# Split first products, three-part sums and a guarded softmax in a convolution and maxout kernel

## The chip, the cores and the metric

The kernel runs on one core of a Trainium2 chip. The metric is the device time of one execution in microseconds (us). TensorE (PE in the profile) multiplies matrices, with its weight loads (PEld) beside it; VectorE (DVE) does elementwise work and reductions, ScalarE (ACT) activations and copies out of PSUM; GpSimd (POOL) and SyncE (SP) mostly issue transfers.

## The reference, cut to what matters

There are 8 x 4160 tokens of 192 features, in 8 heads of 24. Each token has 7 taps of weights per head, and a mixture of the last 7 tokens is formed with the softmax of these weights. Then comes a maxout layer with 1024 hidden columns.

```python
w = exp(weight_gen - max(weight_gen)); w = w / (sum(w) + 1e-9)     # 7 taps
y[s, h] = sum over k of w[s, h, k] * x_padded[s + k, h]            # 6 rows of zeros ahead
out = maximum(y @ w1, y @ w2) @ w_out                              # 192 -> 1024 -> 192
```

## The kernel before

**Layout.** Each of the 128 partitions holds 260 consecutive tokens, called columns. They form 17 batches: sixteen of 16 columns and one of 4. A batch is cut into units: four units of 4 columns in batches 0 and 1 (units 0 to 7), two of 8 columns later (units 8 to 35; unit 36 has 4). A unit of n columns gives n tiles of hidden work for TensorE, 260 in all. Tiles are taken in groups of two up to tile 16 and of three after that.

**Softmax.** No maximum is subtracted. For each batch, `exp_sum` (ACT, L135) makes exponentials, `red` (DVE, L147) sums the 7 taps, `ln` (ACT, L151) takes the logarithm, `shift` (DVE, L156) subtracts it from the weights, and `weights` (ACT, L167) takes the exponentials of the result, as bf16.

**Mixture.** `mul` (DVE, L182) multiplies 7 shifted views of x by the weights of one piece (4 or 8 columns) into `m_t`. For units 0 to 7, `sum_transpose` (PE, L248) adds the taps and transposes them in one go, by matmuls with an identity matrix, and ACT copies the result out (L255). From unit 8 on, `adds` (DVE, L198, L204, L207) adds the taps, a DMA transpose on SP (L216) turns the unit around, and a one-column copy on POOL (L224, tile `gate`) waits for its landing, with the next loads of x and of weights queued behind it on POOL. Stores of results that were held back are issued on SP right behind a transpose.

**Maxout.** max(a, b) = a + relu(b - a), so the weights are prepared as `wd` = w2 - w1 (`w_diff`, L584 to L591) and `w10` = w1 @ w_out. `hid_tile` (PE, L299) makes the differences of a tile, `relu` (ACT, L309) takes them out of PSUM, `out_first` and `out_second` (PE, L351, L339) add both products, `evac` (ACT, L395) copies the results and SP stores them (L409, the last one at L386 on SP and ACT).

**Order.** The schedule is manual: each engine works through the instructions in the order in which the program writes them. In the long stretch, `extra` puts DVE's work beside tiles: `mul`, then `adds` with a `beside` step ahead of the additions. A unit at the start of a batch has the three parts of a `shift` there, the other has two parts of a `red`. ACT's softmax steps come when a tile is reached: the table `due` is filled from defaults and from the table `AT` (an entry `('l', 8, 0): 95` places `ln` of batch 8 at tile 95; `X` is `exp_sum`, `W` is `weights`). Long steps can be put off by one group unless the group is in `NOW`.

**Start.** SP loads batch 0's weights, the halo (the six columns ahead), columns 0 to 3 of x, the first halves of w1 and w2, columns 4 to 7, then the rest. `mul(0, 0)` waits for columns 0 to 3; PE meanwhile runs `keep_warm` (L615, matmuls whose result is not used). The loads of columns 8 to 15 on POOL wait for `mul(0, 0)`.

Of the kernel before, what the change touches and what calls it, by code (L numbers as in the profile page):

```python
# [9 lines left out]
FP32 = mybir.dt.float32  # L10
# [13 lines left out]
def kernel(  # L24
# [19 lines left out]
    CPP = B * S // P  # L44
    RPB = P // B
    G = D // H
    assert RPB * CPP == S
# [27 lines left out]
    consts = ctx.enter_context(tc.tile_pool(name="consts", bufs=1))  # L75
    pwg = ctx.enter_context(tc.tile_pool(name="pwg", bufs=4))
    pxb = ctx.enter_context(tc.tile_pool(name="pxb", bufs=2))
    pe_ = ctx.enter_context(tc.tile_pool(name="pe", bufs=2))
    psm = ctx.enter_context(tc.tile_pool(name="psm", bufs=3))
    pm = ctx.enter_context(tc.tile_pool(name="pm", bufs=1))  # L80
    pen = ctx.enter_context(tc.tile_pool(name="pen", bufs=2))
    py = ctx.enter_context(tc.tile_pool(name="py", bufs=2))
    pyt = ctx.enter_context(tc.tile_pool(name="pyt", bufs=6))
    prd = ctx.enter_context(tc.tile_pool(name="prd", bufs=7))
    first_ps = ctx.enter_context(ExitStack())
    ps = {k: first_ps.enter_context(tc.tile_pool(name="pps_" + k, bufs=2, space=bass.MemoryType.PSUM))
          for k in ("h", "o")}

    def later_ps():

        first_ps.close()
        for k in ("ab", "c", "r"):
            ps[k] = ctx.enter_context(tc.tile_pool(name="pps_" + k, bufs=1, space=bass.MemoryType.PSUM))

    wg_ts, xb_ts, e_ts, s_ts, en_ts, y_ts, yt_ts = {}, {}, {}, {}, {}, {}, {}

# [38 lines left out]
    def part(b, i, of):  # L137
# [3 lines left out]
        return slice(h0, h1), h0 * K, [[K, h1 - h0], [1, K]]  # L141

    def red(b, i=0, of=1):
        if i == 0:
            s_ts[b] = psm.tile([P, BATCHES[b][1] * H], FP32, name="sum_t", tag="sum")
        hs, at, ap = part(b, i, of)
        nc.vector.reduce_sum(out=s_ts[b][:, hs], in_=_sub(e_ts[b], at, ap), axis=AX.X)  # L147

    def ln(b, i=0, of=1):
        s_t = s_ts[b][:, part(b, i, of)[0]]  # L150
        nc.scalar.activation(out=s_t, in_=s_t, func=AF.Ln)  # L151

    def shift(b, i=0, of=1):
        hs, at, ap = part(b, i, of)
        w_t = _sub(wg_ts[b], at, ap)
        nc.vector.tensor_tensor(out=w_t, in0=w_t, in1=_sub(s_ts[b], hs.start, [[1, hs.stop - hs.start], [0, K]]),  # L156
                                op=ALU.subtract)

    def weights(b, o):

        w = dict(pieces(b))[o]
        if b not in en_ts:
            en_ts[b] = pen.tile([P, 16 * WGC * 2], BF16, name="en_t", tag="en")
        J = 2 if w == 4 and b < 2 else 1
        N = w * H // J
        for j in range(J):
            nc.scalar.activation(  # L167
                out=_sub(en_ts[b], (o * WGC + j * N * K) * 2, [[2 * N, K], [2, N], [1, 2]]),
                in_=_sub(wg_ts[b], (o * H + j * N) * K, [[1, K], [K, N], [0, 2]]), func=AF.Exp,
            )  # L170


    def mul(b, o):

        n = dict(pieces(b))[o]
        if n == 4 and b < 2:
            m_out = _sub(m_t, K * o * D, [[64, 2], [P, K * 6], [1, 64]])
            x_in = _sub(xb_ts[b], o * D, [[2 * D, 2], [D, K], [1, 2 * D]])
        else:
            m_out = m_t[:, K * o * D:K * (o + n) * D]  # L180
            x_in = _sub(xb_ts[b], o * D, [[D, K], [1, n * D]])
        return nc.vector.tensor_tensor(  # L182
            out=m_out, in0=x_in,
            in1=_sub(en_ts[b], o * WGC * 2, [[2, K * n * H], [0, G // 2], [1, 2]]),
            op=ALU.mult,
        )
# [51 lines left out]

    def sum_transpose(u, taps=range(K)):

        b, o, n = UNITS[u]
        assert n == 4
        yps = ps["r" if "r" in ps else "o"].tile([P, 1024], FP32, name="yps", tag="op")
        for k in range(6):
            for t in taps:
                for r in range(2):
                    at = (K * o + t * n) * D + k * P
                    nc.tensor.matmul(  # L248
                        yps[:, r * 512 + k * 64:r * 512 + (k + 1) * 64],
                        lhsT=m_t[half(r), at:at + P], rhs=ident[half(r), half(r)],  # L250
                        start=(k == 0 and t == taps[0]), stop=(t == taps[-1]),
                        skip_group_check=True,
                    )
        yt = pyt.tile([P, 8 // 2 * 3 * P], BF16, name="yt", tag="yt")
        yt_of[u] = nc.scalar.copy(out=_sub(yt, 0, [[64, 2], [P, 6], [1, 64]]),  # L255
                                  in_=_sub(yps, 0, [[512, 2], [64, 6], [1, 64]]))
        yt_ts[u] = yt
# [119 lines left out]
    def evac(p, n):  # L377
# [20 lines left out]
        for q in range(p, p + n):  # L398
            u, i, _ = column(2 * q)
            if NU - 7 <= u < NU - 1 and i % 2:  # L400
                stores.append((nc.sync, place(q)[0] - 1, [4 * D, 2], [1, 2 * D]))
            elif u < NU - 7 and i == UNITS[u][2] // 2 - 1:
                stores.append((nc.sync, place(q)[0] - i, [1, 2 * (i + 1) * D]))
            if u == NU - 1:
                stores.append((nc.sync, place(q)[0], [2 * D, 2], [1, D]))
# [104 lines left out]
    msk = consts.tile([P, 1], FP32, name="msk")  # L510
    gate = consts.tile([P, 1], FP32, name="gate")
    o_last = consts.tile([P, 2 * D], FP32, name="o_last")

    with tc.tile_pool(name="pstage", bufs=1) as pstage:
# [57 lines left out]
        for o in (0, 4, 8, 12):  # L572
            weights(0, o)
        nc.vector.tensor_copy(out=xb_ts[0][:, PAD * D:(PAD + 4) * D],
                              in_=xs[:, PAD * D:(PAD + 4) * D])
        first_mul = mul(0, 0)
        w1 = {kind: pstage.tile([P, w], BF16, name="w1" + kind)
              for kind, w in (("E", F), ("T", HF))}

        nc.scalar.copy(out=w1["E"][:, 0:HF], in_=ws["E", 0][:, 0:HF])  # L580
        def w_diff(h, copy):

            c0 = slice(h * HF, (h + 1) * HF)
            nc.vector.tensor_tensor(out=wd[:, c0], in0=ws["E", 1][:, c0], in1=ws["E", 0][:, c0],  # L584
                                    op=ALU.subtract)
            copy(out=wd_at(1, 2, h, 0, HF), in_=wd[0:64, c0])
            copy(out=wd_at(0, 1, h, 0, HF), in_=wd[64:P, c0])
            if h == 0:
                nc.vector.tensor_tensor(out=wd[:, 2 * HF:3 * HF], in0=ws["T", 1], in1=ws["T", 0],
                                        op=ALU.subtract)  # L590
            copy(out=wd_at(1 - h, 1 + h, h, 0, HF), in_=wd[half(h), 2 * HF:3 * HF])  # L591
# [19 lines left out]

        def keep_warm(times):

            for _ in range(times):
                nc.tensor.matmul(warm[:, 0:512], lhsT=ident, rhs=_sub(ident, 0, [[0, 4], [1, P]]),  # L615
                                 start=True, stop=True, skip_group_check=True)

        keep_warm(30)
        w_diff(0, nc.scalar.copy)
        nc.vector.tensor_copy(out=xb_ts[0][:, (PAD + 4) * D:(PAD + 8) * D], in_=xs[:, (PAD + 4) * D:])  # L620
        behind(first_mul, load_x(0, 8, 4))
        load_x(0, 12, 4)
# [4 lines left out]

        sum_transpose(0)
        keep_warm(8)
        mul(0, 4)  # L630


        nc.scalar.copy(out=w1["T"], in_=ws["T", 0])  # L633
# [7 lines left out]
        relu(rd, 1, 1)  # L641
        w_diff(1, nc.vector.tensor_copy)
        sum_transpose(1)
        red(1)
# [51 lines left out]

    pout = ctx.enter_context(tc.tile_pool(name="pout", bufs=1))
    o_t.append(pout.tile([P, 24 * D], FP32, name="o_t", tag="o"))
# [5 lines left out]
    def end_of_1():  # L704
# [15 lines left out]

    NOW = (22, 28, 40, 49, 106)
    AT = {
# [6 lines left out]
        ('W', 3, 0): 22,  # L729
        ('l', 8, 0): 95,  # L730
        ('l', 11, 0): 144,
        ('l', 12, 0): 162,
        ('l', 5, 0): 45,
    }
    due = {}
# [26 lines left out]
    def extra(t):  # L762
# [14 lines left out]
        if s == 8 + later and b + 2 < NB:  # L777
            adds(b + 1, 8, beside=lambda i, of: red(b + 3, i, 2) if b + 3 < NB and i < 2 else None)
        if k == n // 4 - 1 and 7 < u + 1 < NU:
            transpose(u + 1)  # L780

    def steps(g, tiles):
# [3 lines left out]
        for t in tiles:  # L786
            extra(t)

    out_room(OUTS[3])
    go = relay(out_first(OUTS[3]))  # L790
# [3 lines left out]
    for g in range(4, len(GROUPS)):  # L794
        if GROUPS[g][1] == 3 and "c" not in ps:
            later_ps()
        tiles = [t for t in range(GROUPS[g][0], sum(GROUPS[g])) if t >= 16]
        if g == 9:
            behind(relu_of[16], load_x(3, 0, 8))
# [4 lines left out]
        else:  # L804
            hidden(g, OUTS[g], beside=lambda: steps(g, tiles))
    rest_of_results(OUTS[-1])

# [28 lines left out]
```

## Time and profile before

| what | value |
|---|---|
| three timed runs | 409.34, 409.50, 410.65 us; median 409.5 us |
| the profiled execution's own time | 410.25 us |
| its span, first to last instruction | 408.4 us |
| granted TensorE clock | full (1.00) |
| PE busy | 398.9 us (98%) |
| DVE busy | 371.7 us (91%) |
| ACT busy | 357.1 us (87%) |
| POOL busy | 72.5 us (18%) |

The span covers the instructions, and 1.85 us of the profiled execution lie around it (410.25 - 408.4). Busy shares are averages over stages: the start (to about 50 us), the long stretch of equal groups, and the end after DVE's last addition at 378.5 us.

### The profile page before, as it was taken

What the parts mean: (1) busy time and instruction counts of PE and PEld (TensorE: products, weight loads), DVE (VectorE), ACT (ScalarE), POOL (GpSimd) and SP (SyncE); (2) the same over time, 40 slices, a digit from 0 to 9 for tenths busy, and PEclk for the clock granted to TensorE, in tenths of its full rate; (3) what the DMA queues carried; (4) which work ended last, traced back from release to release, by engine and by line L of the source; (5) the groups of instructions that cost most, each with busy time, mean ns of one, the idle gap of its engine ahead of it and who ended that gap; (6) DMA issues with size and microseconds to landing.
All of it is one profiled execution on the core that took longest, in us unless ns stands there. A gap on an engine that the chain in (4) does not pass through costs nothing.

```text
span 408.4 us, 16153 instructions
## 1 busy us (share of the span) xinstructions
PE 398.9 (98%) x7422; PEld 317.6 (78%) x7422; DVE 371.7 (91%) x216; ACT 357.1 (87%) x424; POOL 72.5 (18%) x101
## 2 busy tenths in 40 slices
PE   7899999999999999999999999999999999999996
PEld 2589989777777777777877777777778777777796
DVE  4999999999999999999999999999999999999000
ACT  6799899999899998898998999998999988988872
POOL 0311012212222112121211122220122220210000
PEclk9999999999999999999999999999999999999999
DMA  8958399767658674976786588478648647654514
GB/s 242 218 125 219 75 186 167 168 165 173 147 113 237 151 167 105 244 201 69 234 203 84 123 248 202 65 243 180 128 109 239 169 68 237 154 127 111 145 55 142
DMA packets 62785, 65.70 MB, mean 161 GB/s; under 512 B 47711, under 2 KB 51679, under 8 KB 62718
## 3 DMA queue, kind: packets, MB, share of 16 engines
q1 hardware_dynamic: 54334, 40.54, 36.7%
q0 software_dynamic: 8240, 24.04, 29.9%
q8 instruction: 58, 0.95, 1.0%
q10 hardware_dynamic: 144, 0.10, 0.1%
q14 instruction: 9, 0.07, 0.1%
HBM read 35.96 MB, written 25.56 MB: 151 GB/s over the span
## 4 chain that ended last, share of the span: by engine, by line
PE 91%; ACT 4%; DMA 3%; issue 1%; SPq 0%; DVE 0%; ACTq 0%
PE op_ps L339 41%; PE hd L299 39%; PE op_ps L351 8%; DMA xs<-in_x_dram 3%; ACT rd_t L309 2%; PE hdp L299 1%; PE yps L248 1%; ACT yt L255 1%; ACT w1t L675 0%; ACT e_t L135 0%; ACT en_t L167 0%; DVE xb_t L620 0%; ACT wd L591 0%; ACT w L668 0%; ACT w1T L633 0%
## 5 line engine op out<-in xcount | busy, mean ns | idle before, releaser
L309 ACT ACTIVATE rd_t<-hd 128x1024 bf16<-128x1024 f32 (+1 forms) x206 | 234.7, 1187 | 27.5 <-PE hd L299 26.3
L339 PE MATMUL op_ps<-wo,rd_t 64*128 64x192 bf16 x4160 | 211.4, 243 | 0.1
L339 PEld LDWEIGHTS <-rd_t 64*128 64x128 bf16 x4160 | 181.7, 94 | 15.7 <-ACTq L372 0.3
L299 PE MATMUL hd<-yt,wd 64*128 64x512 bf16 (+1 forms) x1584 | 188.1, 360 | 0.7 <-issue 0.6
L182 DVE TENSOR_TENSOR m_t<-xb_t,en_t 128x10752 bf16<-128x10752 bf16 (+1 forms) x37 | 187.4, 5070 | 0.2
L299 PEld LDWEIGHTS <-wd 64*128 64x128 bf16 x1776 | 94.5, 94 | 43.2 <-issue 2.8
L224 POOL CAST gate<-yt 128x1 f32<-128x1 bf16 x29 | 37.8, 1305 | 264.3 <-DMA yt<-y_t 264.3
L198 DVE TENSOR_TENSOR m_t<-m_t 128x4608 bf16<-128x4608 bf16 (+1 forms) x30 | 74.1, 2470 | 0.1
L395 ACT COPY o_t<-op_ps 128x384 f32<-128x384 f32 (+1 forms) x99 | 57.3, 589 | 12.8 <-PE op_ps L339 12.8
L351 PE MATMUL op_ps<-w,yt 64*128 64x192 bf16 x780 | 56.0, 243 | 0.4 <-ACT w L668 0.4
L351 PEld LDWEIGHTS <-yt 64*128 64x128 bf16 x780 | 38.6, 94 | 16.7 <-issue 1.3
L204 DVE TENSOR_TENSOR m_t<-m_t 128x3072 bf16<-128x3072 bf16 (+1 forms) x29 | 50.0, 1723 | 0.1
L167 ACT ACTIVATE en_t<-wg_t 128x896 bf16<-128x896 f32 (+2 forms) x45 | 35.8, 821 | 0.0
L207 DVE TENSOR_TENSOR y_t<-m_t 128x1536 bf16<-128x1536 bf16 (+1 forms) x29 | 27.3, 941 | 0.5
L114 POOL DMA_DIRECT2D xb_t<-in_x_dram x33 | 17.6, 534 | 32.0 <-ACT rd_t L309 19.8
L147 DVE TENSOR_REDUCE sum_t<-e_t 128x64 f32<-128x448 f32 (+2 forms) x31 | 19.6, 635 | 3.3 <-ACT e_t L135 3.3
L156 DVE TENSOR_TENSOR wg_t<-wg_t,sum_t 128x280 f32<-128x280 f32 (+5 forms) x46 | 22.0, 481 | 0.0
L135 ACT ACTIVATE e_t<-wg_t 128x896 f32<-128x896 f32 (+2 forms) x18 | 16.1, 901 | 2.6 <-DMA wg_t<-in_weight_gen_dram 2.6
L309 ACT ACTIVATE rd_t<-hdp 128x1024 bf16<-128x1024 f32 x16 | 16.3, 1056 | 0.5 <-PE hdp L299 0.4
L299 PE MATMUL hdp<-yt,wd 64*128 64x256 bf16 x192 | 13.2, 270 | 0.7 <-issue 0.5
L615 PE MATMUL warm<-ident 128*128 128x512 bf16 x38 | 10.7, 449 | 2.6 <-DVE ident L562 2.6
L248 PEld LDWEIGHTS <-m_t 64*128 64x128 bf16 x636 | 10.1, 95 | 2.6 <-DVE m_t L182 2.5
(45 smaller groups left out, 65.9 us busy)
## 6 DMA issues: line engine op xcount, KB each, us to landing
out_dram<-o_t SPq DMA_DIRECT2D x22, 768.0 KB, 4.8
xb_t<-in_x_dram POOLq DMA_DIRECT2D x30, 384.0 KB, 5.2
out_dram<-o_t SPq DMA_DIRECT2D x20, 384.0 KB, 3.1
wg_t<-in_weight_gen_dram POOLq DMA_DIRECT2D x14, 448.0 KB, 5.3
xb_t<-xb_t POOLq DMA_DIRECT2D x16, 288.0 KB, 5.4
wg_t<-in_weight_gen_dram SPq DMA_DIRECT2D x2, 448.0 KB, 4.4
xs<-in_x_dram SPq DMA_DIRECT2D x2, 384.0 KB, 7.2
xb_t<-in_x_dram POOLq DMA_DIRECT2D x3, 192.0 KB, 4.4
```

The lines of the kernel that those rows point to most:

```text
L156: nc.vector.tensor_tensor(out=w_t, in0=w_t, in1=_sub(s_ts[b], hs.start, [[1, hs.stop - hs.start], [0, K]]), op=ALU.subtract)
L167: nc.scalar.activation(out=_sub(en_ts[b], (o * WGC + j * N * K) * 2, [[2 * N, K], [2, N], [1, 2]]), in_=_sub(wg_ts[b], (o * H + j * N) * K ...
L182: return nc.vector.tensor_tensor(out=m_out, in0=x_in, in1=_sub(en_ts[b], o * WGC * 2, [[2, K * n * H], [0, G // 2], [1, 2]]), op=ALU.mult,)
L198: nc.vector.tensor_tensor(out=taps(0, 1, 3), in0=taps(0, 1, 3), in1=taps(3, 1, 3), op=ALU.add)
L204: nc.vector.tensor_tensor(out=taps(0, 2, 2), in0=taps(0, 2, 2), in1=taps(1, 5, 2), op=ALU.add)
L207: nc.vector.tensor_tensor(out=_sub(y_ts[b], o * D, [[64, 2], [P, 3 * w // 2], [1, 64]]), in0=taps(0, 1, 1), in1=taps(2, 1, 1), op=ALU.add,)
L224: nc.gpsimd.tensor_copy(out=gate, in_=yt[:, 0:1])
L299: nc.tensor.matmul(hid_out(t, f, j), lhsT=wd_at(j, s, f // 4, f % 4 * P, P), rhs=_sub(yt_ts[u][half(j), :], (s + j) % 3 * P, [[3 * P, w // ...
L309: relu_of[t0] = nc.scalar.activation(out=rd[:, k * 1024:(k + n) * 1024], in_=hd[:, at:at + n * 1024], func=AF.Relu)
L339: return nc.tensor.matmul(op_out(c), lhsT=rd[half(r), k * 1024 + at:k * 1024 + at + P], rhs=wo[half(r), f * D:(f + 1) * D], start=False, s ...
L351: nc.tensor.matmul(op_out(c + j), lhsT=yt_ts[u][half(j), (3 * i + (s + j) % 3) * P:(3 * i + (s + j) % 3 + 1) * P], rhs=w10[half(j), s * D: ...
L395: nc.scalar.copy(out=_sub(o, c % 24 * D, [[D, len(qs)], [h * D, 2], [1, D]]), in_=_sub(tile_, at + (qs[0] - p) * D, [[D, len(qs)], [512, 2 ...
```

## The change

- **First products in two parts.** `weights` of the first two pieces of batch 0 makes taps 0 to 2 and taps 3 to 6 apart. `mul(0, 0)` and `mul(0, 4)` are cut in the same way. Taps 0 to 2 of the first piece read the halo alone, those of the second the halo's neighbours (columns 0 to 3). The first part of `mul(0, 0)` stands ahead of the copy of columns 0 to 3, and the first part of `mul(0, 4)` between the two differences of `w_diff(0)`. The transposing sums are cut alike on PE, and the 30 + 8 warming matmuls become 22 of 512 columns, 12 of 256 and 4 of 512. The load of columns 8 to 15 now waits for the first part of `mul(0, 4)`.
- **Sums in three parts.** In the units that carry a `red`, its three parts stand one ahead of each addition (before: two parts, ahead of the first two). Sums go to two lasting tiles, logarithms to a tile of their own.
- **Places on ACT.** `ln` of batches 8, 11 and 12 goes from tiles 95, 144 and 162 to 97, 147 and 165; `exp_sum` of batch 11 to tile 132, and the group at tile 130 joins `NOW`.
- **Test and second path.** After its last addition DVE takes the largest and smallest of all sums, compares them with 1e18 and 1e-18, and a small transfer on SP and one more reduction make a flag. At the end each engine loads the flag into a register and branches. If it is set, a loop over the 260 columns computes everything again with the maximum subtracted; otherwise the branch passes over it.
- **Stores.** Unit 30 is stored in one transfer, not in two halves. The first block also gets four register moves on POOL (the second path needs them).

```diff
+    sums = [consts.tile([P, 3 * 16 * H], FP32, name="sums")]
...
+        for (t0, t1), j in [(ts, j) for ts in tap_parts(b, o) for j in range(J)]:
             nc.scalar.activation(
...
+        mul(0, 0, 0, 3)
         nc.vector.tensor_copy(out=xb_ts[0][:, PAD * D:(PAD + 4) * D],
                               in_=xs[:, PAD * D:(PAD + 4) * D])
-        first_mul = mul(0, 0)
+        mul(0, 0, 3, K)
...
-        keep_warm(30)
-        w_diff(0, nc.scalar.copy)
+        def first_sums():
+            keep_warm(22)
+            sum_taps(0, range(3), True, False)
+            keep_warm(12, 256)
+            sum_transpose(0, range(3, K), False)
+            began.append(mul(0, 4, 0, 3))
+        w_diff(0, nc.scalar.copy, nc.scalar.copy, first_sums)
...
-        behind(first_mul, load_x(0, 8, 4))
+        behind(began[0], load_x(0, 8, 4))
...
-        sum_transpose(0)
-        keep_warm(8)
-        mul(0, 4)
+        keep_warm(4)
+        sum_taps(1, range(3), True, False)
+        mul(0, 4, 3, K)
...
-    NOW = (22, 28, 40, 49, 106)
+    NOW = (22, 28, 40, 49, 106, 130)
...
-        ('l', 8, 0): 95,
-        ('l', 11, 0): 144,
-        ('l', 12, 0): 162,
+        ('l', 8, 0): 97,
+        ('l', 11, 0): 147,
+        ('l', 12, 0): 165,
         ('l', 5, 0): 45,
+        ('X', 11, 0): 132,
...
-            adds(b + 1, 8, beside=lambda i, of: red(b + 3, i, 2) if b + 3 < NB and i < 2 else None)
+            adds(b + 1, 8, beside=lambda i, of: red(b + 3, i, 3) if b + 3 < NB else None)
...
+    def out_of_range():
+        for i, (op, beyond, limit) in enumerate(((ALU.max, ALU.is_gt, S_MOST), (ALU.min, ALU.is_lt, S_LEAST))):
+            for j in range(2):
+                nc.vector.tensor_reduce(out=ends[:, 2 * i + j:2 * i + j + 1], in_=sums[j], axis=AX.X, op=op)
+            nc.vector.tensor_single_scalar(out=ends[:, 2 * i:2 * i + 2], in_=ends[:, 2 * i:2 * i + 2],
+                                           scalar=limit, op=beyond)
+        nc.vector.tensor_reduce(out=bad, in_=ends, axis=AX.X, op=ALU.max)
+        nc.sync.dma_start(out=bad_row, in_=bad)
+        nc.vector.tensor_reduce(out=flag, in_=bad_row, axis=AX.X, op=ALU.max)
...
+        if g == len(GROUPS) - 3:
+            out_of_range()
...
     rest_of_results(OUTS[-1])
+    fast.close()
+    any_bad = nc.values_load(flag[0:1, 0:1], min_val=0, max_val=1,
+                             skip_runtime_bounds_check_because="a maximum of comparisons, each 0 or 1")
+    with tc.If(any_bad > 0):
...
+            all_again(pg, pgp, pgd)
```

## The prediction

> **What bounds the kernel now.** I read the page first: busy shares, then the chain that ended last.
>
> ```profile
> PE 398.9 (98%) x7422; PEld 317.6 (78%) x7422; DVE 371.7 (91%) x216; ACT 357.1 (87%) x424; POOL 72.5 (18%) x101
> ...
> PE 91%; ACT 4%; DMA 3%; issue 1%; SPq 0%; DVE 0%; ACTq 0%
> ```
>
> TensorE sets the time from about 50 us to the end. So the change can act in three ways: a shorter start, a hole in TensorE's work, a longer end. The timeline of the start shows what TensorE waits for:
>
> ```profile
> 9.08 0.56 DVE L574 CAST xb_t<-xs 128x768 bf16<-128x768 f32 x1 [1.40 <-DMA xs<-in_x_dram]
> 9.75 2.96 DVE L182 TENSOR_TENSOR m_t<-xb_t,en_t 128x5376 bf16<-128x5376 bf16 x1
> ...
> 12.63 0.69 DVE L584 TENSOR_TENSOR wd<-ws1E,ws0E 128x512 bf16<-128x512 f32 x1
> ...
> 13.34 0.62 ACT L586 COPY wd<-wd 64x512 bf16<-64x512 bf16 x1 [2.48 <-DVE wd L584]
> ...
> 16.99 1.02 ACT L309 ACTIVATE rd_t<-hdp 128x1024 bf16<-128x1024 f32 x1
> ```
>
> The number in brackets is the engine's idle time and what ended it. DVE idles until columns 0 to 3 land at 9.06, ACT until DVE's first difference; from there to 28 us ACT never pauses (8.00 of 8.00 busy in 20 to 28).
>
> Next I took, unit by unit, the landing of the transpose (the `gate` copy on POOL) and TensorE's first use of it. DVE needs 11.82 to 11.85 us per unit of eight tiles, TensorE 11.52, so the lead shrinks: 10.2 us at unit 8, 5.4 at unit 20, 2.2 to 3.4 at units 26 to 31. At unit 32 nothing is left:
>
> ```profile
> 339.49 1.42 SPq L216 DMA_TRANSPOSE yt<-y_t  x1
> ...
> 341.00 1.31 SPq L409 DMA_DIRECT2D out_dram<-o_t  x2
> ...
> 344.33 1.47 PE L299 MATMUL hd<-yt,wd 64*128 64x512 bf16 x12
> ...
> 344.93 0.18 POOL L224 CAST gate<-yt 128x1 f32<-128x1 bf16 x1 [10.69 <-DMA yt<-y_t]
> ```
>
> The seventh of these twelve matmuls, at 344.98, is the first on unit 32. Its transpose, with two stores issued behind it on SP, took 5.3 us; units without such stores land in 3.65 to 3.9. The lead is 0.04 us, so any lateness of DVE there goes straight into TensorE.
>
> **The start, part by part.** `mul` of 5376 elements takes 2.95 us and of 10752 5.75, so 0.52 ns per element and 0.15 per instruction: the parts take 1.35 and 1.75. Part one of `mul(0, 0)` needs the halo alone and fits in the 1.40 us in which DVE idled (8.0 to 9.35); the copy then ends at 9.9 instead of 9.64, part two at 11.7 instead of 12.71. `w_diff`'s first difference starts at 11.65 instead of 12.63 (its operand lands at 11.26). ACT's chain from L586 is without a pause and starts 0.98 earlier, and the first `relu` comes at 16.0 instead of 16.99. Part one of `mul(0, 4)` fills 12.3 to 13.6, where DVE waited for columns 4 to 7 (13.96); part two ends at about 16.7 instead of 17.66. Four more `weights` instructions cost ACT 0.5 us (224 elements take 0.41, with a pitch of 0.30), hidden because ACT's next step waits for the first half of w1 until 10.22. TensorE's own additions (the recut warming) lie in its waits. What can spoil it: the load of columns 8 to 15 is issued at 13.9 instead of 13.02, and the halo of batch 1 lands at 26.14 for a `mul` at 26.95, which would want it at 25.95. Bounds: 0 (this late load eats all) to 1.5 (pauses of 0.5 us further on close too). **Taken: -1.0**, the shift of ACT's chain.
>
> POOL gets four register moves ahead of the first instructions. No such row exists; POOL's memsets start 0.03 us apart. Bounds 0 to 0.3, **taken +0.14**.
>
> **The long stretch.** A red of 64 columns takes 0.53 us from start to start, so the three parts (40, 48, 40 columns) take 0.36, 0.41 and 0.36. Together that is more than two parts, but the pair of additions that has no step between takes 1.78 us from start to start against 1.67 with one, so a step there saves 0.11; in sum a unit goes from 11.85 to about 11.80. That is 0.05 per batch for DVE.
>
> More weight lies on `ln`. The first of the moved ones:
>
> ```profile
> 161.41 0.34 ACT L151 ACTIVATE sum_t<-sum_t 128x128 f32<-128x128 f32 x1
> ...
> 166.63 0.45 DVE L156 TENSOR_TENSOR wg_t<-wg_t,sum_t 128x280 f32<-128x280 f32 x1
> ...
> 167.36 1.07 ACT L167 ACTIVATE en_t<-wg_t 128x896 bf16<-128x896 f32 x1
> 168.29 1.91 ACT L309 ACTIVATE rd_t<-hd 128x2048 bf16<-128x2048 f32 x1
> ```
>
> The changed order puts `ln` of batch 8 right behind this `weights` step, so at 168.29, ending at 168.64. DVE wants to start its `shift` at 166.63 and needs that logarithm: it stands for 2.0 us, and the additions, the transpose and the next `mul` queue up behind it. For batch 12 it is the same: `weights` at 262.35, `ln` from 263.28 to 263.63, `shift` wanted at 262.11, so 1.56 late against the old clock. The two do not add up: both are lateness against TensorE's clock, which places ACT's steps, and the later one counts. For batch 11 `ln` comes in time. The `exp_sum` moved to tile 132 takes away a stall of 0.71 at 202.92, which only gives back lateness.
>
> From 263 to unit 32 DVE recovers 0.05 in each of the batches with a red: 1.56 falls to about 1.4. Unit 32 then lands at 346.2 and is wanted at 344.98. **TensorE stands 1.25 us.** The shift of the start cancels here, since ACT, placed by TensorE, and DVE, released by ACT, move together. Bounds: 0, if that transpose took 3.65 as most do, to 1.5 with nothing recovered. Taken: 1.25, since every unit with two stores behind its transpose (17, 22, 27, 32) needed 4.8 to 5.4. The joint `exp_sum` of batch 11 in a `NOW` group puts about 0.9 us ahead of a `relu`; TensorE is buffered by a group there: **+0.1** (0 to 0.2).
>
> **The end.** The test is issued when DVE is done (378.5) and the flag is ready by about 393: hidden. What counts is the last instructions:
>
> ```profile
> 404.87 0.48 ACT L383 COPY o_last<-op_ps 128x384 f32<-128x384 f32 x1
> 405.38 0.34 SPq L386 DMA_DIRECT2D out_dram<-o_last  x1
> 405.38 0.37 ACTq L386 DMA_DIRECT2D out_dram<-o_last  x1
> ```
>
> These stores land at about 407.4 and the span ends at 408.3. Behind its store SP now loads the flag into a register, compares, branches past the second path, and goes through its closing waits, twelve by about 0.06 us (ten now). No row shows a register load. Bounds: 0.03, the pitch of POOL's small instructions, and 2.0, a whole 96 KB store from issue to landing. I take 1.0, between them, since it moves four bytes but has to come back to the sequencer. With 0.4 for two branches (bounds 0.1 to 0.8): 405.72 + 1.0 + 0.4 + 0.74 = 407.86, against 407.53 now: **+0.35** (0 to 3); up to 407.5 it hides behind the stores. The Trainium skill, in "DMA: Bandwidth & Descriptors", Latency and other measured facts, gives a floor of about 600 ns for such a load; by that the end would cost nothing, and no row here shows it.
>
> **Sum**, against the profiled execution's own 410.25: -1.0 + 0.14 + 0.1 + 1.25 + 0.35 = +0.84, or 411.1. That execution lies 0.75 above the median run, so on the median's scale 410.3.
>
> **Rivals.** (1) *The start's gain survives*: no stall at unit 32, because its transpose lands early or the two stores, issued at another distance, do not collide with it. For it: units 28 to 31 land in 3.65 to 3.9. Against: all four two-store units were slow. Time: 410.3 - 1.25 = 409.1, or 408.6 with 1.5 at the start.
> (2) *Slower by the branch*: the taken branch finds its target not yet loaded, and the engine has to fetch instructions before it can close. The target lies 37 (SP) to 107 (PE) instructions ahead. The page's instruction queues show what a fetch costs: 58 packets at 1.0% of sixteen engines' span (65 us) are 1.1 us each, those of the other queue 0.7. One or two of these, and the register load near its upper bound, add 1.5 to 2.4: 411.8 to 412.7. It decides as soon as load, branch and fetch exceed 1.8 us, the time that the stores cover. For it: every engine branches. Against: the targets are near. The Trainium skill's "Runtime: NRT & Kernel Launch", Instruction fetch mechanics, says that a taken branch whose target is outside the current two-page window forces a fetch; by this rule the short jump should mostly be free, and no run here shows one.
> (3) *The change does not do what it says*, and the second path runs: 260 rounds with three transfers each of no less than 2 us in a row is over 1.5 ms. The sums of seven exponentials are nowhere near 1e18.
>
> **How the numbers follow.** About 0.3% (1.23 us) can be told from no change here. Forecast 0.42, rival 1 0.30, rival 2 0.27, rival 3 0.01. Faster than 408.3 needs rival 1 with the start's upper bound: 0.12, and 0.02 of the forecast. Slower than 410.7: rivals 2 and 3 (0.28), and 0.12 from the forecast with a start that gives less or an end that costs more. The rest, 0.46, is the same. The range goes from 408.4 (rival 1 with the better start) to 412.7 (rival 2's upper end).
>
> **What would show it.** In the changed kernel: a first `mul` part at about 8.0 and the first `relu` at 16.0 (else the start failed); `shift` of batch 8 waiting on ACT's `ln` for 2 us near 167, and of batch 12 near 262; TensorE idle by 1.25 us at the first matmul of unit 32, released by the transpose (else rival 1); SP reaching its closing waits by about 407 (else rival 2). The forecast is wrong if TensorE has no hole near 345, or the span runs on for over 4 us behind the last store's issue.

## The result, and the profile after

The changed kernel is slower: 415.45 us (median of six runs, 412.8 to 417.18) beside 409.96 us, a ratio of 1.0132 with a 95% interval of 1.0107 to 1.0157. The ratios here and below come from runs paired on one chip and need not equal the quotient of the medians. The execution that was profiled was the fastest of the six: 412.8 us, span 411.1, against 410.25 and 408.4 before.

The page after, busy shares, chain and two groups:

```profile
PE 398.7 (97%) x7422; PEld 317.6 (77%) x7422; DVE 377.0 (92%) x239; ACT 357.7 (87%) x428; POOL 168.7 (41%) x101
...
DVE 53%; PE 24%; DMA 9%; ACT 6%; issue 5%; SPq 1%; POOL 1%; DVEq 0%; ACTq 0%; POOLq 0%
...
L236 POOL CAST gate<-yt 128x1 f32<-128x1 bf16 x29 | 133.7, 4612 | 173.4 <-DMA yt<-y_t 173.4
L194 DVE TENSOR_TENSOR m_t<-xb_t,en_t 128x10752 bf16<-128x10752 bf16 (+3 forms) x39 | 187.8, 4818 | 6.9 <-DMA xb_t<-xb_t 3.3
```

The same two groups before:

```profile
L182 DVE TENSOR_TENSOR m_t<-xb_t,en_t 128x10752 bf16<-128x10752 bf16 (+1 forms) x37 | 187.4, 5070 | 0.2
L224 POOL CAST gate<-yt 128x1 f32<-128x1 bf16 x29 | 37.8, 1305 | 264.3 <-DMA yt<-y_t 264.3
```

TensorE's work is unchanged, but the chain that ended last is now DVE's (53%, before 0%). POOL went from 72.5 to 168.7 us busy, and nearly all of the increase lies in 29 copies of one column: the gate takes 4612 ns on average, before 1305. DVE's multiplication waited 6.9 us, 6.1 of it in three units for x; before, all of its waits came to 0.2.

The timeline of unit 27 shows what a gate does in that time. Before, the copy arrived at 285.28, when the multiplication was nearly done, went through as the shift began, and the load of x followed at once:

```profile
280.11 5.75 DVE L182 TENSOR_TENSOR m_t<-xb_t,en_t 128x10752 bf16<-128x10752 bf16 x1
285.28 0.63 POOL L224 CAST gate<-yt 128x1 f32<-128x1 bf16 x1 [10.22 <-DMA yt<-y_t]
285.78 0.44 DVE L156 TENSOR_TENSOR wg_t<-wg_t,sum_t 128x280 f32<-128x280 f32 x1
285.84 0.53 POOL L114 DMA_DIRECT2D xb_t<-in_x_dram  x1
```

After:

```profile
283.49 5.75 DVE L194 TENSOR_TENSOR m_t<-xb_t,en_t 128x10752 bf16<-128x10752 bf16 x1
287.51 13.58 POOL L236 CAST gate<-yt 128x1 f32<-128x1 bf16 x1 [9.01 <-DMA yt<-y_t]
289.15 0.44 DVE L164 TENSOR_TENSOR wg_t<-wg_t,ln_t 128x280 f32<-128x280 f32 x1
289.51 2.55 DVE L210 TENSOR_TENSOR m_t<-m_t 128x4608 bf16<-128x4608 bf16 x1
...
294.43 0.95 DVE L219 TENSOR_TENSOR y_t<-m_t 128x1536 bf16<-128x1536 bf16 x1
295.30 5.75 DVE L194 TENSOR_TENSOR m_t<-xb_t,en_t 128x10752 bf16<-128x10752 bf16 x1
300.97 0.43 DVE L153 TENSOR_REDUCE later_sums<-e_t 128x40 f32<-128x280 f32 x1
301.03 0.53 POOL L118 DMA_DIRECT2D xb_t<-in_x_dram  x1
...
302.09 1.81 POOL L236 CAST gate<-yt 128x1 f32<-128x1 bf16 x1
```

The copy sits on POOL for 13.58 us, through eight DVE steps, and ends when the first part of a sum starts (300.97). Everything from the multiplication to that point is a TENSOR_TENSOR with two inputs in SBUF; the sum has one. The load of x behind the gate goes out 15.2 us later than before (301.03 against 285.84); 3.4 of that is the lateness that the whole unit already had.

What that costs is seen where the lead is used up, 190 to 218 us:

```profile
190.97 12.44 POOL L236 CAST gate<-yt 128x1 f32<-128x1 bf16 x1 [7.32 <-DMA yt<-y_t]
...
203.35 0.53 POOL L118 DMA_DIRECT2D xb_t<-in_x_dram  x1
...
204.41 1.81 POOL L236 CAST gate<-yt 128x1 f32<-128x1 bf16 x1
...
206.69 0.55 POOL L108 DMA_DIRECT2D wg_t<-in_weight_gen_dram  x1
...
212.26 5.76 DVE L194 TENSOR_TENSOR m_t<-xb_t,en_t 128x10752 bf16<-128x10752 bf16 x1 [2.77 <-ACT rd_t L329]
215.14 0.95 ACT L139 ACTIVATE e_t<-wg_t 128x896 f32<-128x896 f32 x1 [2.69 <-DMA wg_t<-in_weight_gen_dram]
...
217.74 0.42 PE L371 MATMUL op_ps<-w,yt 64*128 64x192 bf16 x6 [2.85 <-ACT o_t L415]
```

x is issued at 203.35 and DVE stands 2.77 us for it. (The bracket names ACT, but the record of DVE's wait on the two x transfers ends at 212.2.) The weights behind the next gate land at 215.1; `exp_sum` stands 2.69 us for them with the `relu` of the hidden tiles queued behind it on ACT, and TensorE stands 2.85 us. From there on little lead is left.

### The profile page after: what moved, and what is told of

It reads as the page before. It is cut to its first block, busy times and chain, and to the rows that moved or that the text cites. A ratio compares the mean times of both kernels' runs of the same rounds, so it can differ in the third digit from the quotient of the medians.

```text
span 411.1 us, 16200 instructions
## 1 busy us (share of the span) xinstructions
PE 398.7 (97%) x7422; PEld 317.6 (77%) x7422; DVE 377.0 (92%) x239; ACT 357.7 (87%) x428; POOL 168.7 (41%) x101
## 4 chain that ended last, share of the span: by engine, by line
DVE 53%; PE 24%; DMA 9%; ACT 6%; issue 5%; SPq 1%; POOL 1%; DVEq 0%; ACTq 0%; POOLq 0%
DVE m_t L194 24%; DVE m_t L210 12%; PE op_ps L359 12%; PE hd L319 9%; DVE m_t L216 8%; DVE y_t L219 4%; DMA yt<-y_t 3%; ACT rd_t L329 3%; DVE wg_t L164 2%; DVE later_sums L153 2%; PE op_ps L371 2%; DMA wg_t<-in_weight_gen_dram 2%; DMA xb_t<-xb_t 2%; DMA ws1T<-in_moe_w_dram 2%; PE hdp L319 1%
## 5 line engine op out<-in xcount | busy, mean ns | idle before, releaser
L236 POOL CAST gate<-yt 128x1 f32<-128x1 bf16 x29 | 133.7, 4612 | 173.4 <-DMA yt<-y_t 173.4
L194 DVE TENSOR_TENSOR m_t<-xb_t,en_t 128x10752 bf16<-128x10752 bf16 (+3 forms) x39 | 187.8, 4818 | 6.9 <-DMA xb_t<-xb_t 3.3
L415 ACT COPY o_t<-op_ps 128x384 f32<-128x384 f32 (+1 forms) x99 | 57.1, 587 | 11.9 <-PE op_ps L359 11.9
L179 ACT ACTIVATE en_t<-wg_t 128x896 bf16<-128x896 f32 (+4 forms) x49 | 36.0, 769 | 0.1
L219 DVE TENSOR_TENSOR y_t<-m_t 128x1536 bf16<-128x1536 bf16 (+1 forms) x29 | 27.1, 935 | 0.1
L164 DVE TENSOR_TENSOR wg_t<-wg_t,ln_t 128x280 f32<-128x280 f32 (+5 forms) x46 | 22.0, 480 | 0.2 <-ACT ln_t L159 0.2
L153 DVE TENSOR_REDUCE later_sums<-e_t 128x40 f32<-128x280 f32 (+4 forms) x40 | 18.1, 453 | 0.0
L641 PE MATMUL warm<-ident 128*128 128x512 bf16 (+1 forms) x38 | 9.8, 421 | 2.9 <-DVE ident L586 2.9
```

What stands on the lines that cost most here:

```text
L164: nc.vector.tensor_tensor(out=w_t, in0=w_t, in1=_sub(l_ts[b], hs.start, [[1, hs.stop - hs.start], [0, K]]), op=ALU.subtract)
L179: nc.scalar.activation(out=_sub(en_ts[b], (o * WGC + (J * t0 + j * (t1 - t0)) * N) * 2, [[2 * N, t1 - t0], [2, N], [1, 2]]), in_=_sub(wg_t ...
L194: return nc.vector.tensor_tensor(out=m_out, in0=x_in, in1=_sub(en_ts[b], (o * WGC + t0 * n * H) * 2, [[2, (t1 - t0) * n * H], [0, G // 2], ...
L219: nc.vector.tensor_tensor(out=_sub(y_ts[b], o * D, [[64, 2], [P, 3 * w // 2], [1, 64]]), in0=taps(0, 1, 1), in1=taps(2, 1, 1), op=ALU.add,)
L236: nc.gpsimd.tensor_copy(out=gate, in_=yt[:, 0:1])
L415: nc.scalar.copy(out=_sub(o, c % 24 * D, [[D, len(qs)], [h * D, 2], [1, D]]), in_=_sub(tile_, at + (qs[0] - p) * D, [[D, len(qs)], [512, 2 ...
```

## The experiments

Theory A: the change moved nearly all tiles by 2144 bytes, and whether a shift lets the gate pass hangs on addresses (modulo 512 bytes). Theory B: the changed order of DVE's instructions holds the gate. Theory C is the prediction's: late logarithms. The first four runs set them against each other.

**Addresses, in the changed kernel.**

```diff
+    pad = consts.tile([P, 104], FP32, name="pad")
     o_last = consts.tile([P, 2 * D], FP32, name="o_last")
```

> A tile of 416 bytes per partition, which nothing uses, is put ahead of o_last, so that every later tile lies at the same address modulo 512 as in the kernel before; no instruction changes. Theory A (addresses: the gate copy on POOL reads SBUF and competes with DVE's two-input instructions; whether the shift lets it pass hangs on where the tiles lie, which the change moved by 2144 bytes): no gate copy is held for more than 2 us, and the time falls from 415.5 to 409.5 to 411. Theory B (the changed order of instructions holds the gate): some 7 gate copies of 11 to 14 us remain, and 413 to 417. Theory C (the prediction: ln comes late): no change, 413 to 417, DVE waiting on ln for over 1 us.

Measured: 413.38 us, 1.0115 (1.0066 to 1.0165); eight gates of 10.7 to 13.6 us. Theory A is out on this side.

**Addresses, in the kernel before** (the same with 24 columns).

> The kernel before with 96 unused bytes per partition ahead of o_last, so that the later tiles lie at the changed kernel's addresses modulo 512; no instruction changes. Theory A (addresses): several gate copies are held for 11 to 14 us and the time rises from 410.0 to 412 to 417. Theories B and C: no gate copy above 2 us, 409.5 to 410.8.

Measured: 409.12 us, 1.0009 (0.998 to 1.0038), no gate above 2.7 us. Out on this side too, as far as addresses modulo 512 go.

**A gate that reads nothing.**

```diff
-        nc.sync.dma_start_transpose(
+        turned = nc.sync.dma_start_transpose(
...
-        nc.gpsimd.tensor_copy(out=gate, in_=yt[:, 0:1])
+        behind(turned, nc.gpsimd.memset(gate, 0.0))
```

> The changed kernel with the gate made a memset that waits for the same transpose, so that POOL's instruction reads nothing from SBUF. If the gate's read is what is locked out (A and B): every gate takes well under 1 us, the loads behind it come in time, DVE no longer waits for x, and the time is 409 to 411. If something else holds POOL: gates stay long, 413 to 417. Theory C: 413 to 417 with short gates.

Measured: 410.78 us, 1.0045 (1.0022 to 1.0068). The group of the page:

```profile
L236 POOL MEMSET gate<- 128x1 f32 x29 | 2.8, 98 | 289.2 <-DMA yt<-y_t 289.2
```

All 29 take 98 ns beside the same DVE work, and the multiplication's waits fall from 6.9 to 0.9 us. So it is the read that is locked out, and the lockout is what costs: of the 1.32% some 0.45% is left. The Trainium skill, in "SBUF — State Buffer", Who interferes with whom, says that a DVE instruction with two SBUF inputs contends with a GpSimd instruction that reads SBUF and not with one that only writes it, and that a reduction does not contend. By that rule the copy should be held by every multiplication, shift and addition and pass at the sums, and a memset never be held. The memset (98 ns) and the held copies agree, but in the kernel before the copy also passed between a multiplication and a shift (unit 27 above), where no sum stands.

**Sums in two parts again.**

```diff
-            adds(b + 1, 8, beside=lambda i, of: red(b + 3, i, 3) if b + 3 < NB else None)
+            adds(b + 1, 8, beside=lambda i, of: red(b + 3, i, 2) if b + 3 < NB and i < 2 else None)
```

> The changed kernel with the sums in two parts, as before. Theory B, in the form that the three parts hold the gate: no gate above 2 us and 409.5 to 411. Theory A: some 5 to 9 held gates as in the changed kernel, 413 to 417.

Measured: 410.19 us, 1.0021 (1.0004 to 1.0038), no gate above 2.0 us. Theory B holds so far: the three parts do it, although they stand in other units than those in which the gate is held.

**The three parts alone, in the kernel before** (the same line, the other way round).

> The kernel before with one edit: the sums in three parts, one ahead of each addition. Theory B (with a step ahead of every addition DVE never pauses within a batch, and POOL's gate copy, which reads SBUF, is then locked out through the whole of a unit whose steps all have two SBUF inputs): some 6 to 10 gate copies of 11 to 14 us, x arriving late, 412 to 417 us. If the hold needs something else of the change as well: no gate above 2 us and 409 to 410.

Measured: 412.59 us, 1.007 (1.0041 to 1.01); seven gates of 10.5 to 13.6 us. This part of the change is enough.

What do three parts change ahead of the next unit? Before, the second and third addition follow each other directly, and the third waits for the second on its own engine:

```profile
277.45 1.75 DVE L204 TENSOR_TENSOR m_t<-m_t 128x3072 bf16<-128x3072 bf16 x1
279.23 0.96 DVE L207 TENSOR_TENSOR y_t<-m_t 128x1536 bf16<-128x1536 bf16 x1
```

After, the third sum stands between:

```profile
280.54 1.74 DVE L216 TENSOR_TENSOR m_t<-m_t 128x3072 bf16<-128x3072 bf16 x1
282.21 0.49 DVE L153 TENSOR_REDUCE later_sums<-e_t 128x48 f32<-128x336 f32 x1
282.62 0.94 DVE L219 TENSOR_TENSOR y_t<-m_t 128x1536 bf16<-128x1536 bf16 x1
```

From start to start the second addition takes 1.78 us before and 1.67 after. That is why the group of the third addition had 0.5 us of idle time on the page of before (L207) and has 0.1 after (L219). With a sum in between, the pause is gone. The next runs ask whether the pause, the number of instructions, or an unbroken run of two-input steps decides.

**Three parts with the pause.**

```diff
+            adds(b + 1, 8, beside=lambda i, of: red(b + 3, i, 3) if b + 3 < NB and i < 2 else None)
+            if b + 3 < NB:
+                red(b + 3, 2, 3)
```

> The changed kernel with three parts, but the third one behind the third addition, so that the second and third addition follow each other with the pause of 0.11 us again; the number of DVE's instructions is that of the changed kernel. Theory B (the pause is what gives POOL its turn): no gate above 2 us, 410 to 411. If the number of instructions or of sums in a batch decides: held gates remain, 413 to 417.

Measured: 410.38 us, 1.0002 (0.9977 to 1.0027), no gate above 2.4 us. A sum now also stands behind the third addition, so this run alone does not single out the pause.

**A one-column step between the third addition and the multiplication.**

```diff
             adds(b + 1, 8, beside=lambda i, of: red(b + 3, i, 3) if b + 3 < NB else None)
+            if b + 3 < NB:
+                nc.vector.memset(tiny, 0.0)
```

> The changed kernel with a memset of one column on DVE behind the third addition of each unit with sums: no pause between additions, but one more instruction per batch (15). Theory B (pause): held gates remain, 413 to 417. If an even or odd number of instructions per batch decides: no gate above 2 us, 410 to 411.

Measured: 410.8 us, 1.0021 (0.9996 to 1.0046), no gate above 2.7 us. My form of theory B (the pause between the additions) falls: there is none here and the gate passes. Left were the number of instructions per batch and the unbroken run.

**The same step outside the run** (behind the multiplication of the units with sums), and **inside it** (behind the multiplication of the units with shifts).

> The changed kernel with a memset of one column on DVE between the multiplication and the first part of the sums, in the units with sums: 15 instructions per batch as in the run with the memset behind the third addition, but the stretch from the third addition to the end of the next unit is the changed kernel's own. If the unbroken run of two-input steps decides: held gates of 11 to 14 us remain in the units with shifts, 412 to 417. If the number of instructions decides: no gate above 3 us, 410 to 411.

> The changed kernel with the same memset between the multiplication and the first part of the shift, in the units with shifts. If the unbroken run decides: the memset breaks it right behind the multiplication, the gate passes there (1.8 us or less, none above 3), 410 to 411. If the run is decided ahead of the multiplication: held gates remain, 412 to 417.

Measured: outside, 417.42 us, 1.0189 (1.0137 to 1.0241), with eight gates of 10.7 to 13.6 us; inside, 409.96 us, 1.0004 (0.9984 to 1.0023), no gate above 2.6 us. Unit 27 of both, outside first:

```profile
283.93 5.75 DVE L194 TENSOR_TENSOR m_t<-xb_t,en_t 128x10752 bf16<-128x10752 bf16 x1
287.95 13.58 POOL L236 CAST gate<-yt 128x1 f32<-128x1 bf16 x1 [9.02 <-DMA yt<-y_t]
289.60 0.43 DVE L164 TENSOR_TENSOR wg_t<-wg_t,ln_t 128x280 f32<-128x280 f32 x1
```

```profile
281.20 5.75 DVE L194 TENSOR_TENSOR m_t<-xb_t,en_t 128x10752 bf16<-128x10752 bf16 x1
285.25 1.74 POOL L236 CAST gate<-yt 128x1 f32<-128x1 bf16 x1 [9.04 <-DMA yt<-y_t]
286.88 0.44 DVE L164 TENSOR_TENSOR wg_t<-wg_t,ln_t 128x280 f32<-128x280 f32 x1
286.90 0.06 DVE L806 MEMSET tiny<- 128x1 f32 x1
```

A step of 0.06 us in the right place is worth 1.8%. The count does not decide; an unbroken run does. All four kernels with held gates can be counted together, in the eleven units with shifts from 11 to 31. Where the third addition started right behind the sum and the multiplication 0.864 to 0.867 us behind that, with no wait ahead of the shift, 27 of 28 gates were held, for 11.9 to 13.7 us. Where DVE stood for x or a logarithm in that stretch, once for only 0.03 us, none of 16 was. Beside this range, unit 9 was held in all four (10.5 to 11.7 us), and unit 33, where the sum is shorter, passed in the one kernel without a pause there (1.77 us).

**The other parts.** Four runs price the rest; the two with a memset also look for a version that beats both kernels.

```diff
 # split_only: the changed kernel less the test and the second path, and with
-        ('l', 8, 0): 97,
-        ('l', 11, 0): 147,
-        ('l', 12, 0): 165,
+        ('l', 8, 0): 95,
+        ('l', 11, 0): 144,
+        ('l', 12, 0): 162,
-        ('X', 11, 0): 132,
-    NOW = (22, 28, 40, 49, 106, 130)
+    NOW = (22, 28, 40, 49, 106)
-            adds(b + 1, 8, beside=lambda i, of: red(b + 3, i, 3) if b + 3 < NB else None)
+            adds(b + 1, 8, beside=lambda i, of: red(b + 3, i, 2) if b + 3 < NB and i < 2 else None)
 # after_red2_places: the same with the test and the second path
 # split_red3_memset: split_only with three parts and the gate as a memset
 # before_memset: the kernel before with the gate as a memset
```

> Of the change only the split first products (with the sums' new tiles and unit 30's single store) is left: sums in two parts, ln, exp_sum and NOW as before, no test and no second path. By the prediction's term the start gives 1.0: 408.8 beside 409.8 for the kernel before. By the profiles so far (the first relu at 16.2 to 17.5 us in three kernels with whole products, 16.4 to 17.5 in seven with split ones) the split gives nothing that can be told: 409.4 to 410.

> The changed kernel with the sums in two parts and ln, exp_sum and NOW as before; the test and the second path stay. Against the first kernel of this call it prices the test, the branch and the four register moves: +0.3 by the last instructions of the profiles, +0.14 for the moves, so 0.2 to 0.7 slower than that one (rival 2 of the prediction: over 1.5 slower). Against the run with two parts and the changed places (1.0021 times the kernel before) it prices the places: by the prediction 1.25, by the profile of that run, where TensorE stood 0.41 at unit 32, some 0.4.

> Split products, sums in three parts and the gate as a memset; places of ln, exp_sum and NOW as before; no test and no second path. If the gate's read is all that makes three parts slow, this is no slower than two parts: 409 to 409.8, and with DVE 0.05 us shorter per batch it keeps a little more lead at unit 32. If three parts have a cost of their own: over 410.5.

> The kernel before with the gate as a memset and nothing else. There the gate was held for 1.3 us on average; the loads behind it go out 1 to 2 us earlier in each unit. If those loads had room (no mul waited for x): 409.4 to 410, no difference that can be told. If the gate's hold cost lead: up to 0.5 faster.

Measured, in this order: 409.69 us, 0.9985 (0.9965 to 1.0006); 410.44 us, 1.0007 (0.9984 to 1.003); 410.62 us, 1.0007 (0.9982 to 1.0032); 409.74 us, 0.9995 (0.9972 to 1.0017). None can be told from the kernel before, so nothing here beats both. Test, branch and register moves come to some 0.9 us (1.0007 less 0.9985; expected 0.2 to 0.7) with intervals that overlap. The places of `ln` and `exp_sum` come to some 0.6 (1.0021 with two parts and the changed places, less 1.0007; expected 0.4), again with intervals that overlap. The third run lies where its expectation spoke of a cost of the three parts' own (over 410.5). The three runs with three parts in which the copy passed (1.0002 to 1.0021, beside 1.0021 with two parts) speak against such a cost, but some 0.9 us (1.0007 less 0.9985) is not excluded.

**The memset with the old places of `ln`** (tiles 95, 144, 162; `exp_sum` at 132 as changed).

> The changed kernel with the gate as a memset and ln of batches 8, 11 and 12 at their old tiles (95, 144, 162). Taken from the run with the memset alone (410.8) and its stall of 2.2 us on ln at unit 17, which ended as lateness of TensorE: DVE waits under 0.5 us for ln in all, unit 32 has a lead of over 1 us, and the time falls by 1 to 1.5 us, to 409.3 to 409.8; with the gate never locked out it may come below the kernel before (409.4). If the places of ln cost nothing: 410.5 to 411.

Measured: 410.55 us, 1.0018 (0.999 to 1.0045); the stand for `ln` near 168 is gone, but a sum stood 0.8 us for `exp_sum` at 203. The gain expected, 1 to 1.5 us, is 0.2 by the medians and 1.1 by the ratios (1.0045 less 1.0018, intervals overlapping): inconclusive.

## Why the prediction was wrong, step by step

**What bounds the kernel** was right: TensorE, with a lead that runs out near unit 32. That is why lateness on DVE and POOL had a price.

**The sums in three parts** are the step that failed. The term itself was right: DVE's unit with sums went from 11.85 to 11.79 us. Left out was what else changed: with the pause filled by the third part, POOL was no longer let through one unit later. The prediction counted the effect on DVE alone and none for POOL's queue. In the runs the part costs 1.1% (1.0132 less 1.0021), or 0.7% in the kernel before. None of the three rivals had POOL in it. The page of before held a hint: a copy of one column that takes 0.18 us alone (units 17, 32) had a mean of 1305 ns, so it was waiting in nearly every unit, with the loads queued behind it.

**The start** was put at -1.0. The profiles shown:

```profile
8.42 1.36 DVE L194 TENSOR_TENSOR m_t<-xb_t,en_t 128x2304 bf16<-128x2304 bf16 x1 [0.34 <-ACT en_t L179]
9.69 0.55 DVE L599 CAST xb_t<-xs 128x768 bf16<-128x768 f32 x1
...
12.03 0.69 DVE L609 TENSOR_TENSOR wd<-ws1E,ws0E 128x512 bf16<-128x512 f32 x1
...
16.39 1.01 ACT L329 ACTIVATE rd_t<-hdp 128x1024 bf16<-128x1024 f32 x1
```

The first `relu` is 0.60 earlier, not 0.99 (0.85 with the register moves counted in, as here). The mis-sized term is part one's place at 8.0: it waits for ACT's first weights, which stand behind ACT's scaling of the halo. In the other profiles the halo landed later and part one began at up to 9.5; then the copy of columns 0 to 3 waits for part one instead of its load, and the gain is lost. Over all profiles the first `relu` comes at 16.98 us on average with whole products (four, 16.18 to 17.46) and at 16.80 with split ones (twelve, 16.23 to 17.51). The run with the split alone allows 0.2 slower to 1.4 faster. A single profiled start was too little to price it from: the load's own spread is as large as the term. Of the late load that the prediction named as able to spoil the start, 0.27 us was seen: the halo of batch 1 landed at 26.36, and the multiplication that wanted it stood for it. The register moves took 0.24 (SP's first load at 0.98, before 0.74; 0.74 again in the run with the split alone, which has no moves), predicted 0.14.

**The places of `ln`**: the mechanism was right, and it shows where the gate is not held. In the run with two parts:

```profile
166.76 1.05 ACT L179 ACTIVATE en_t<-wg_t 128x896 bf16<-128x896 f32 x1
167.68 0.32 ACT L159 ACTIVATE ln_t<-later_sums 128x128 f32<-128x128 f32 x1
...
168.03 0.45 DVE L164 TENSOR_TENSOR wg_t<-wg_t,ln_t 128x280 f32<-128x280 f32 x1 [1.80 <-ACT ln_t L159]
```

DVE stood 1.80 us (with the memset 2.12), predicted 2.0, and a further 0.56 at batch 12. The hole at unit 32 was over-sized:

```profile
340.70 2.51 SPq L228 DMA_TRANSPOSE yt<-y_t  x1
...
345.00 0.82 PE L319 MATMUL hd<-yt,wd 64*128 64x512 bf16 x6 [0.41 <-DMA yt<-y_t]
```

0.41 us, predicted 1.25: that transpose landed after 4.3 us, not 5.3. Its two stores went out 2.6 us behind it, in the kernel before 1.5; rival 1 had named that distance, and no run tests it. In the changed kernel itself DVE stood for `ln` 0.24 us at batch 12 and not at batch 8, since it was later than that already. The stall of 0.71 us for `exp_sum` that its new place was to take away was still there where DVE was not late (0.80 near 203, in the run with the memset and the old places of `ln`).

**The end** held: from the last store's issue to the end of the span 3.18 us against 3.02, so +0.16 for +0.35. The records show SP's register load at 0.54 us, where 1.0 was taken, and the first closing wait 0.46 behind its branch. Rival 2 is out. The Trainium skill's floor of about 600 ns ("DMA: Bandwidth & Descriptors", Latency and other measured facts) lies a little above the 0.49 to 0.56 us that the loads of the five engines took here.

The sum, which has nothing for POOL's queue, was +0.84, and the run with two parts gave 1.0021, some 0.9 us. That agreement is partly luck: its terms were off in both directions (start less good, hole smaller).

**Still open** is why a pause ahead of a run keeps it passable to its end. In the kernel before, the shift also starts 5.67 us behind the start of the multiplication, just as in the held units, and yet the gate passes there. The runs show when the gate is held, not what decides between the two engines. One of the 28 gates passed without a visible pause, and why is not known. Why single runs of the changed kernel spread over 4 us was not tried either. Late loads whose landing varies may be a reason; the three longest runs also had the lowest granted clock (0.994 to 0.996, the others 0.998 to 1.0).

## What to carry to other kernels

Before filling a pause on a busy engine, ask who uses that pause: list what the neighbouring queues hold at that moment, and what is queued behind it. A tiny instruction that serves only as a gate should read nothing; if a copy of one column takes seven times its own time in the profile (here 1305 ns for 0.18 us), it is waiting for more than its input, and a change to another engine's order can turn 1 us into 13. Price a gain at the start from several profiles, as the landing of the loads spreads by as much as the gain.

## What the runs showed of the hardware that was not expected

A POOL copy of one column waited for up to 13.7 us while DVE ran steps with two SBUF inputs back to back, and was let through at once by a DVE step of 0.06 us without such inputs. Whether POOL got its turn at a boundary between two such steps went, with one exception in the 44 cases counted, with whether DVE had paused since the third addition of the unit before, or, in the kernels with two parts, just ahead of it: pauses of some 0.03 us were enough, while the steps at the boundary itself were the same and 5.67 us apart in both cases. POOL's memset beside the same steps was never held (98 ns, 29 of 29).
